# One numerator moved from the FFN chunks to the first down phase, whose tile pairs take their output projection last

## The chip, the cores and the metric

The kernel runs on one core of a Trainium2 chip. The metric is device time in microseconds (us), the median of repeated executions. TensorE appears in the profile as PE (matmuls) and PEld (weight loads), VectorE as DVE, ScalarE as ACT, GpSimd as POOL, and the queue that issues DMAs as SPq.

## The reference

A linear attention with softmax feature maps and a gated FFN share one input x of 2048 tokens by 640, and a per-token gate g mixes their outputs.

```python
qkv = x @ wqkv                       # 32 heads of 20
phi = concat[softmax(. @ w_phi), softmax(-. @ w_phi)]   # of q and of k
kv, z = phi_k^T v, sum(phi_k)        # per head
o = (phi_q kv) / (phi_q z + 1e-6)
a = o @ wo
b = (gelu(x @ w_gate) * (x @ w_up)) @ w_down            # F = 1728
out = g * a + (1 - g) * b,  g = sigmoid((x * gate_w).sum(-1))
```

## The kernel before, in words

Tokens are cut into 16 tiles of 128 and four blocks of four tiles (512 tokens). The attention state comes first (the first 80 us or so): projections, exponentials, their normalization and the key-value sums. Then `ffn` (line 752 on) runs two kinds of phase.

**Gate and up, `gateups(b)`**, four times, one for each block. Each runs 14 chunks of 128 FFN columns (`gateup`): five matmuls for the gate and five for the up product, 128 rows deep and 512 columns wide, into two PSUM banks, the pair (0, 1) or the pair (6, 7) in turn. ACT takes the gelu, DVE multiplies and leaves `hT`, the hidden values transposed.

**Down, `downs(b)`**, four times. Two tile pairs of a block follow each other, both through `down_pair` (line 696). A pair has an output of 640 columns, cut into two halves of 320 (h = 0 and 1); each half of each tile has a bank of its own: half 0 uses banks 0 and 1, half 1 uses banks 6 and 7, and the second pair, and the first pair of the next block, use the same four banks again. Every matmul here is only 64 rows deep, so two of them lie in the array beside each other: row half r = 0 works for one tile of the pair and r = 1 for the other. One such couple is a step here, and after each step the generator yields. A bank is filled in two turns: the opening, in which row half r works for tile r, and the closing, in which they change tiles, because the two row halves must not write one bank together. Before the closing writes a bank, PE waits for its own last opening matmul there (the key `turn`). The steps are 14 or 13 chunks of the down product (`wd_sb`, `hT`) and 5 chunks of the output projection (`wo_sb`, `goT`), which adds the attention's result to the same sums.

The order of a pair, before: opening down steps of half 0, then half 1 (14 + 14), opening projection steps (5 + 5), then the closing of half 0 with 13 down and 5 projection steps, its eviction, and the closing of half 1 with as many, its eviction. `evac` (line 722) evicts two banks, those of the two tiles, one after the other on ACT with the gate as scale (line 730), and issues the output DMA on SP after half 1.

**Numerators, `num(t)`** (line 647), one for each tile: 22 matmuls, 64 rows deep and 66 columns wide (line 662), into banks 2 to 5; then eleven DVE operations (lines 677 to 690), which read these banks and leave `Og`; then a transposing DMA on SP (line 693) that makes `goT`, which the projection steps of that tile read. `num` is called from hooks: `first_nums` after chunks of `gateups(1)`, and the dictionary `side` of `downs`, which maps a yield's count to a tile. Before, tiles 0 and 1 are made after chunks 4 and 8 of `gateups(1)`, and each down phase makes four at yields 1, 31, 61 and 91 (the last phase two). A phase has 148 yields.

The order within each engine is the program's; a scheduler object (`_Sched`, line 22) only adds the semaphore waits.

Of the kernel before, what the change touches and what calls it, by code (L numbers as in the profile page):

```python
# [107 lines left out]
class _Kernel:  # L108
# [6 lines left out]
    NFC = 14  # L115
# [279 lines left out]
    def mm(self, bank, c0, n, lhs, rhs, first, fin, reads):  # L395
        self.sc.op("pe", lambda e: e.matmul(  # L396
            self.ps[:, bank * 512 + c0:bank * 512 + c0 + n], lhs, rhs, start=first, stop=fin),
            reads=reads, writes=[("ps", bank)], signal=fin)
# [294 lines left out]
        sc.dma("sp", lambda e: e.dma_start_transpose(self.goT[:, gs, :, :], self.Og[:, sl, :]),  # L693
               reads=[("Og", sl)], writes=[("goT", gs)], guard=old)

    def down_pair(self, t0, banks, widths):

        sc = self.sc
        ts = (t0, t0 + 1)
        NFC, KD = self.NFC - 1, self.KD  # L700
        nw = len(widths)
        hk = t0 // 4
        last = t0 + 2 == self.NT
        os_ = t0 % 4

        def mm(r, j, h, c, opens, x, n):
            t = ts[j]
            tt, gs, bk, w0, a = t % 4, t % 8, banks[h][j], sum(widths[:h]), 64 * r
            w, end = widths[h], x == n - 1
            if c <= NFC:  # L710
                lhs, rhs = self.hT(hk, c)[a:a + 64, tt * P:(tt + 1) * P], self.wd_sb[a:a + 64, c, w0:w0 + w]
                rd = [("hT", hk, c), "wd"] if c < NFC else [("hT", hk, 13, r), ("wd13", r)]
            else:
                k = c - NFC - 1
                lhs, rhs = self.goT[a:a + 64, gs, k, :], self.wo_sb[a:a + 64, k, w0:w0 + w]
                rd = [("goT", gs), "wo"]
            sc.op("pe", lambda e: e.matmul(self.bank(bk, w), lhs, rhs, start=opens and x == 0, stop=end and not opens,  # L717
                                           skip_group_check=True),
                  reads=rd, writes=[("ps", bk)] + ([("turn", bk)] if end else []), signal=end,
                  after=[("turn", bk)] if x == 0 and not opens else ())  # L720

        def evac(h):
            w0, w = sum(widths[:h]), widths[h]
            for j in (0, 1):
                bk, dst, g = banks[h][j], self.outsb[:, os_ + j, w0:w0 + w], self.Gm[:, ts[j]:ts[j] + 1]
                rd, wr = [("ps", bk), "Gm"], [("outsb", os_ + j, h)]
                if last and j == 1:
                    sc.op("dve", lambda e: e.tensor_scalar(dst, self.bank(bk, w), g, None, op0=ALU.mult), reads=rd, writes=wr)
                else:
                    sc.op("act", lambda e: e.activation(dst, self.bank(bk, w), AF.Copy, scale=g), reads=rd, writes=wr)  # L730
            if last:
                hs, c0, c1 = [h], w0, w0 + w
            elif h == nw - 1:
                hs, c0, c1 = range(nw), 0, self.D
            else:
                return
            if t0 < self.TB:
                rows = self.out[0:self.BT, :].rearrange("(p j) n -> p j n", j=self.TB)[:, t0:t0 + 2, :]
            else:
                rows = self.out[t0 * P:(t0 + 2) * P, :].rearrange("(j p) n -> p j n", p=P)  # L740
            sc.dma("sp", lambda e: e.dma_start(rows[:, :, c0:c1], self.outsb[:, os_:os_ + 2, c0:c1]),
                   reads=[("outsb", os_ + j, k) for j in (0, 1) for k in hs], writes=[("out", t0, h)])

        wos = [NFC + 1 + k for k in range(KD)]
        opening = list(range(NFC + 1)) + wos
        for part in (range(NFC + 1), range(NFC + 1, len(opening))):
            for h in range(nw):
                for x in part:
                    for r in (0, 1):
                        mm(r, r, h, opening[x], True, x, len(opening))  # L750
                    yield None
        closing = list(range(NFC)) + wos
        for h in range(nw):
            for x, c in enumerate(closing):
                for r in (0, 1):
                    mm(r, 1 - r, h, c, False, x, len(closing))
                if c == closing[-1]:
                    evac(h)
                yield None

    NUMB = 2
    oldk = [("Ek", k, s) for k in range(5) for s in (0, 1)] + [(w, k) for w in ("Ekc", "Ekp") for k in range(5)] + [
# [5 lines left out]
    def ffn(self):  # L768
        self.gn = 0
        self.pn = 0  # L770
        pairs = [(0, 1), (6, 7)]

        def gateups(b, after):
            for idx, c in enumerate([0, 1, 13] + list(range(2, 13))):
                self.gateup(b, c, pairs[self.pn % 2])
                self.pn += 1
                after(idx)

        def downs(b, side):
            p = [pairs[(self.pn + k) % 2] for k in (0, 1)]  # L780
            n = 0
            for t in (4 * b, 4 * b + 2):
                final = t + 2 == self.NT
                for _ in self.down_pair(t, p + [(2, 3)] if final else p, (256, 256, 128) if final else (320, 320)):
                    n += 1
                    if n in side:
                        self.num(side[n])

        def state(idx):
            if idx < 4:  # L790
                self.gram(12 + idx)
            if idx == 3:
                self.kv_state()
                self.gates()

        def first_nums(idx):
            if idx in (4, 8):
                self.num(idx // 4 - 1)

        def none(idx):  # L800
            pass
        at = (1, 31, 61, 91)
        gateups(0, state)
        gateups(1, first_nums)
        gateups(2, none)
        gateups(3, none)
        for b in range(self.NB):
            downs(b, {at[k]: 4 * b + 2 + k for k in range(4 if b < 3 else 2)})


def bass_gated_mix__linear_kernel_hedgehog__geglu_ffn__prompt_kernel(
# [41 lines left out]
```

## Time and profile before

| what | value |
|---|---|
| median of 3 runs (lowest, highest) | 284.77 us (284.77, 285.49) |
| the profiled execution's own time | 284.86 us |
| its span | 283.5 us |
| granted TensorE clock | 1.00 |
| busy: PE, DVE, ACT, POOL | 280.3, 172.8, 104.8, 13.2 us |
| gateups(1) and its two numerators | about 107 to 138 us of the span |
| down phase of block 0 | 195.9 to 217.4 us |
| a down phase with four numerators | 21.48 us |

The profiled execution took 1.36 us more than its span; a change of the time is taken to be a change of the span. In a line of the timeline, the first number is the start in us from the span's start, the second how long the group lasted, then engine, line of the code, operation, tiles written and read, shape and count; brackets at the end give the idle time before it and what ended it. Matmuls are pipelined: a row of one lasts longer than the distance to the next, so distances between starts are what counts.

### The profile page before, as it was taken

What the parts mean: (1) busy time and instruction counts of PE and PEld (TensorE: products, weight loads), DVE (VectorE), ACT (ScalarE), POOL (GpSimd) and SP (SyncE); (2) the same over time, 40 slices, a digit from 0 to 9 for tenths busy, and PEclk for the clock granted to TensorE, in tenths of its full rate; (3) what the DMA queues carried; (4) which work ended last, traced back from release to release, by engine and by line L of the source; (5) the groups of instructions that cost most, each with busy time, mean ns of one, the idle gap of its engine ahead of it and who ended that gap; (6) DMA issues with size and microseconds to landing.
All of it is one profiled execution on the core that took longest, in us unless ns stands there. A gap on an engine that the chain in (4) does not pass through costs nothing.

```text
span 283.5 us, 6887 instructions
## 1 busy us (share of the span) xinstructions
PE 280.3 (99%) x2922; PEld 174.7 (62%) x2922; DVE 172.8 (61%) x325; ACT 104.8 (37%) x191; POOL 13.2 (5%) x67
## 2 busy tenths in 40 slices
PE   8999999999999999999999999999999999999996
PEld 5677777777754444444444444445777777777786
DVE  1369999999995332667242334325883883884801
ACT  4357888887852223222332223231112112012011
POOL 7500101110000000000000000000000000000000
DMA  8994398989999500011000000000133233232221
GB/s 227 189 219 91 60 198 179 192 180 165 171 250 353 146 0 0 2 23 24 2 0 0 0 2 0 0 0 2 25 50 85 58 44 76 72 44 76 73 73 49
DMA packets 58922, 24.11 MB, mean 85 GB/s; under 512 B 50954, under 2 KB 58378, under 8 KB 58890
## 3 DMA queue, kind: packets, MB, share of 16 engines
q1 hardware_dynamic: 58224, 23.63, 38.8%
q8 instruction: 23, 0.38, 0.6%
q10 hardware_dynamic: 666, 0.03, 0.2%
q14 instruction: 9, 0.07, 0.1%
HBM read 9.04 MB, written 2.62 MB: 41 GB/s over the span
## 4 chain that ended last, share of the span: by engine, by line
PE 94%; SPq 3%; DMA 2%; issue 0%; ACT 0%
PE ps L396 61%; PE ps L717 28%; PE ps L662 2%; DMA xT<-in_A_x_dram 2%; PE ps L506 2%; SPq L229 1%; SPq L245 1%; PE ps L374 1%; SPq L233 1%; SPq L225 0%; ACT outsb L730 0%
## 5 line engine op out<-in xcount | busy, mean ns | idle before, releaser
L396 PE MATMUL ps<-xT,wu_sb 128*128 128x512 bf16 x260 | 64.6, 379 | 0.0
L396 PE MATMUL ps<-xT,wg_sb 128*128 128x512 bf16 x260 | 64.6, 379 | 0.0
L633 ACT ACTIVATE gl<-ps 128x512 bf16<-128x512 f32 x52 | 31.1, 598 | 76.0 <-PE ps L396 73.8
L635 DVE TENSOR_TENSOR hT<-ps,gl 128x512 bf16<-128x512 f32 x39 | 26.7, 691 | 43.2 <-PE ps L396 43.2
L717 PE MATMUL ps<-wd_sb,hT 64*128 64x320 bf16 x648 | 48.4, 296 | 0.0
L396 PEld LDWEIGHTS ps<-xT,wu_sb 128*128 128x128 bf16 x260 | 25.4, 98 | 30.9 <-DVE hT L635 0.4
L396 PEld LDWEIGHTS ps<-xT,wg_sb 128*128 128x128 bf16 x260 | 25.0, 98 | 29.4
L730 ACT ACTIVATE outsb<-ps,Gm 128x320 bf16<-128x320 f32 (+2 forms) x31 | 14.6, 516 | 71.7 <-PE ps L717 71.7
L396 PE MATMUL ps<-w,xT 128*128 128x304 bf16 (+3 forms) x280 | 40.6, 296 | 0.3 <-DMA xT<-in_A_x_dram 0.3
L717 PEld LDWEIGHTS ps<-wd_sb,hT 64*128 64x128 bf16 x648 | 30.9, 94 | 12.2 <-issue 0.4
L396 PEld LDWEIGHTS ps<-w,xT 128*128 128x128 bf16 x280 | 26.4, 97 | 10.2 <-DMA xT<-in_A_x_dram 0.5
L717 PE MATMUL ps<-wo_sb,goT 64*128 64x320 bf16 (+2 forms) x340 | 26.5, 288 | 0.0
L495 DVE TENSOR_TENSOR Ek<-Ek,Dk 128x1320 bf16<-128x1320 bf16 x16 | 24.5, 1532 | 0.5
L688 DVE TENSOR_TENSOR O<-ps,RH 128x640 bf16<-128x640 f32 x32 | 24.8, 817 | 0.0
L486 DVE TENSOR_REDUCE Dk<-Ek 128x66 f32<-128x1320 bf16 x16 | 24.3, 1520 | 0.0
L396 PE MATMUL ps<-wq,xT 128*128 128x304 bf16 x160 | 23.3, 292 | 0.0
L453 ACT ACTIVATE Eqt<-ps 128x627 bf16<-128x627 f32 x32 | 20.5, 694 | 6.5 <-PE ps L396 6.5
L453 ACT ACTIVATE Ek<-ps 128x627 bf16<-128x627 f32 x32 | 20.5, 694 | 2.8 <-PE ps L396 2.6
L635 DVE TENSOR_TENSOR xT<-ps,gl 128x512 bf16<-128x512 f32 x13 | 9.0, 692 | 18.2 <-PE ps L396 18.2
L717 PEld LDWEIGHTS ps<-wo_sb,goT 64*128 64x128 bf16 x340 | 15.9, 94 | 5.3
L396 PEld LDWEIGHTS ps<-wq,xT 128*128 128x128 bf16 x160 | 15.0, 98 | 4.5
L717 PE MATMUL ps<-wd_sb,xT 64*128 64x320 bf16 (+2 forms) x270 | 16.0, 269 | 0.0
(77 smaller groups left out, 180.1 us busy)
## 6 DMA issues: line engine op xcount, KB each, us to landing
out_dram<-outsb SPq DMA_DIRECT2D x7, 320.0 KB, 2.3
wd_sb<-in_B_w_down_dram SPq DMA_DIRECT2D x1, 2080.0 KB, 10.6
wg_sb<-in_B_w_gate_dram SPq DMA_DIRECT2D x5, 224.0 KB, 4.0
wu_sb<-in_B_w_up_dram SPq DMA_DIRECT2D x5, 224.0 KB, 3.4
wg_sb<-in_B_w_gate_dram SPq DMA_DIRECT2D x5, 192.0 KB, 3.7
wu_sb<-in_B_w_up_dram SPq DMA_DIRECT2D x5, 192.0 KB, 3.3
w<-in_A_wqkv_dram SPq DMA_DIRECT2D x5, 160.0 KB, 4.0
wo_sb<-in_A_wo_dram SPq DMA_DIRECT2D x1, 800.0 KB, 9.6
```

The costliest lines, as they stand in the source:

```text
L229: sc.dma("sp", lambda e: e.dma_start_transpose(T[:, :, :], self.wqkv[:, c0:c0 + D]), writes=[key])
L396: self.sc.op("pe", lambda e: e.matmul(self.ps[:, bank * 512 + c0:bank * 512 + c0 + n], lhs, rhs, start=first, stop=fin), reads=reads, writ ...
L453: self.sc.op("act", lambda e: e.activation(dst, src, AF.Exp, scale=scale), reads=[("ps", b), ("ps", b + 1)], writes=[(name, sl, s)])
L486: self.sc.op("dve", lambda e: e.tensor_reduce(self.Dk[:, se, 0, :].rearrange("p (u h) -> p u h", h=self.HG), self.k_view(se), AX.X, ALU.ad ...
L495: sc.op("dve", lambda e: e.tensor_tensor(v, v, R.rearrange("p (u h) -> p u h", h=self.HG).unsqueeze(3).to_broadcast([P, 2 * self.G, self.H ...
L506: self.sc.op("pe", lambda e: e.matmul(self.bank(b)[:, c:c + n], self.Ek[:, se, g * P:(g + 1) * P], va[:, w * g:w * g + n], start=(t == 0 a ...
L633: sc.op("act", lambda e: e.activation(self.gl[:, slot, :], self.bank(banks[0]), AF.Gelu_apprx_tanh), reads=[("ps", banks[0])], writes=[("g ...
L635: sc.op("dve", lambda e: e.tensor_tensor(hT, self.bank(banks[1]), self.gl[:, slot, :], ALU.mult), reads=[("ps", banks[1]), ("gl", slot)], ...
L662: sc.op("pe", lambda e: e.matmul(self.ps[:, o:o + n], self.Eq[a:a + 64, g, t * P:(t + 1) * P], self.KV[a:a + 64, g, 0:n], start=(g in (0, ...
L688: dve(lambda e, o=o, f=f, s=s: e.tensor_tensor(o, V[s][:, :, 0:DH], f, ALU.mult), rb + [key(6 + s)], [("O", s, sl)], guard=old)
L717: sc.op("pe", lambda e: e.matmul(self.bank(bk, w), lhs, rhs, start=opens and x == 0, stop=end and not opens, skip_group_check=True), reads ...
L730: sc.op("act", lambda e: e.activation(dst, self.bank(bk, w), AF.Copy, scale=g), reads=rd, writes=wr)
```

## The change

Tile 0's numerator goes to the hook after chunk 8 of `gateups(1)`, the one after chunk 4 is gone, and the first down phase makes five numerators, tiles 1 to 5, at yields 1, 31, 61, 91 and 121. The other phases keep theirs. In the first down phase, for both tile pairs (`late=True`), the order becomes: opening down (14 + 14), closing down (13 + 13), opening projection (5 + 5), closing projection (5 + 5), with each half's eviction after its last step. The couple of row halves changes tiles three times in a pair, not once. The other three down phases keep their order.

```diff
-    def down_pair(self, t0, banks, widths):
+    def down_pair(self, t0, banks, widths, late=False):
...
-        def mm(r, j, h, c, opens, x, n):
+        def mm(r, j, h, c, begins, ends, opens, stops):
...
-            sc.op("pe", lambda e: e.matmul(self.bank(bk, w), lhs, rhs, start=opens and x == 0, stop=end and not opens,
-                                           skip_group_check=True),
-                  reads=rd, writes=[("ps", bk)] + ([("turn", bk)] if end else []), signal=end,
-                  after=[("turn", bk)] if x == 0 and not opens else ())
+            sc.op("pe", lambda e: e.matmul(self.bank(bk, w), lhs, rhs, start=opens, stop=stops, skip_group_check=True),
+                  reads=rd, writes=[("ps", bk)] + ([("turn", bk)] if ends else []), signal=ends,
+                  after=[("turn", bk)] if begins and not opens else ())
...
-        opening = list(range(NFC + 1)) + wos
-        for part in (range(NFC + 1), range(NFC + 1, len(opening))):
+        odown, cdown = list(range(NFC + 1)), list(range(NFC))
+        if late:
+            parts = [(0, odown), (1, cdown), (0, wos), (1, wos)]
+        else:
+            parts = [(0, odown), (0, wos), (1, cdown + wos)]
+        for k, (swap, steps) in enumerate(parts):
+            fin = k == len(parts) - 1
+            begins = k == 0 or parts[k - 1][0] != swap
+            ends = fin or parts[k + 1][0] != swap
             for h in range(nw):
-                for x in part:
+                for x, c in enumerate(steps):
+                    top, bot = x == 0, x == len(steps) - 1
                     for r in (0, 1):
-                        mm(r, r, h, opening[x], True, x, len(opening))
+                        mm(r, r ^ swap, h, c, begins and top, ends and bot, k == 0 and top, fin and bot)
+                    if fin and bot:
+                        evac(h)
                     yield None
-        closing = list(range(NFC)) + wos
-        for h in range(nw):
-            for x, c in enumerate(closing):
-                for r in (0, 1):
-                    mm(r, 1 - r, h, c, False, x, len(closing))
-                if c == closing[-1]:
-                    evac(h)
-                yield None
...
-                for _ in self.down_pair(t, p + [(2, 3)] if final else p, (256, 256, 128) if final else (320, 320)):
+                for _ in self.down_pair(t, p + [(2, 3)] if final else p, (256, 256, 128) if final else (320, 320), b == 0):
...
         def first_nums(idx):
-            if idx in (4, 8):
-                self.num(idx // 4 - 1)
+            if idx == 8:
+                self.num(0)
...
         at = (1, 31, 61, 91)
+        first = (1, 31, 61, 91, 121)
...
-            downs(b, {at[k]: 4 * b + 2 + k for k in range(4 if b < 3 else 2)})
+            if b:
+                downs(b, {at[k]: 4 * b + 2 + k for k in range(4 if b < 3 else 2)})
+            else:
+                downs(b, {first[k]: 1 + k for k in range(5)})
```

More of the change, by code (lines that the diff above doesn't have):

```diff
@@ L704, in down_pair @@
         os_ = t0 % 4
-        def mm(r, j, h, c, opens, x, n):
+        def mm(r, j, h, c, begins, ends, opens, stops):
             t = ts[j]
             tt, gs, bk, w0, a = t % 4, t % 8, banks[h][j], sum(widths[:h]), 64 * r
-            w, end = widths[h], x == n - 1
+            w = widths[h]
             if c <= NFC:
```

## The prediction

> **What bounds the kernel now.** I read the page's busy shares first, then the waits, then the timelines of the two stages that are touched.
>
> ```profile
> PE 280.3 (99%) x2922; PEld 174.7 (62%) x2922; DVE 172.8 (61%) x325; ACT 104.8 (37%) x191; POOL 13.2 (5%) x67
> ...
> PE 94%; SPq 3%; DMA 2%; issue 0%; ACT 0%
> ```
>
> PE is busy in 99% of the span, and the chain that ended last is PE for 94%. The list of waits gives PE one wait on a DMA (0.3 us) in the whole program and none in the down phases. So the change is worth what it does to the distances between PE's instructions: what PE no longer issues or drains is gained in full, and each new wait of PE is paid in full.
>
> What a numerator costs among FFN chunks (timeline of PE in gateups(1)):
>
> ```profile
> 115.91 1.24 PE L396 MATMUL ps<-xT,wu_sb 128*128 128x512 bf16 x5
> 117.08 0.51 PE L662 MATMUL ps<-KV,Eq 64*128 64x66 bf16 x22
> 117.53 1.25 PE L396 MATMUL ps<-xT,wg_sb 128*128 128x512 bf16 x5
> ```
>
> Five matmuls of a chunk take 1.08 us from start to start (118.62 less 117.53 is 1.09). Without the numerator the gate matmuls would have started at 116.99; they start at 117.53, 0.54 later, and the next five another 0.01 later. ACT agrees: its idle time before that chunk's gelu is 2.11 us where all others have 1.56, so 0.55 us.
>
> What one costs among down steps, which are 64 rows deep as it is, and what follows a half's last step there:
>
> ```profile
> 203.51 0.84 PE L717 MATMUL ps<-wo_sb,goT 64*128 64x320 bf16 x10
> 204.19 0.84 PE L717 MATMUL ps<-wd_sb,hT 64*128 64x320 bf16 x10
> 204.87 0.50 PE L662 MATMUL ps<-KV,Eq 64*128 64x66 bf16 x22
> 205.22 1.25 PE L717 MATMUL ps<-wd_sb,hT 64*128 64x320 bf16 x16
> ```
>
> Five steps take 0.68 us, so a step is 0.136; the numerator moves the next step by 205.22 - 204.87 = 0.35 us. The phase agrees: 148 steps of 0.136 and four times 0.35 make 21.5 us, and it takes 21.48.
>
> **The change part by part.**
>
> The numerator that moves. Removed: 0.55 us in gateups(1), since DVE's eleven operations delay no chunk that PE waits for (PE idles nowhere there). Added: 0.35 us in downs(0). Together -0.20 us.
>
> The order of a pair: as many steps as before (28 + 26 + 10 + 10 = 74), each with the same shapes, so nothing by count. More changes of tile, each with a wait for PE's own last matmul in the bank: the nearest is 5 steps back (0.68 us), and the same wait over 5 steps stands in the profile before (opening projection of half 1 between, closing starts at 201.75) without a gap in the rhythm. I cost it at nothing; if it cost what a matmul row lasts beyond its slot (0.30 - 0.14) it would be 0.16 us each, eight times, but no row hints at it.
>
> The eviction. This is the part that costs. Half 0's banks are evicted after its last step, and the next pair starts with half 0, on the same banks. Before, 18 steps of half 1 lie between (2.4 us); after, 5 steps (0.68 us). The eviction, from ACT's timeline:
>
> ```profile
> 204.42 0.95 ACT L730 ACTIVATE outsb<-ps,Gm 128x320 bf16<-128x320 f32 x2 [8.92 <-PE ps L717]
> 207.21 0.95 ACT L730 ACTIVATE outsb<-ps,Gm 128x320 bf16<-128x320 f32 x2 [1.84 <-PE ps L717]
> ```
>
> Let T be the start of half 0's last step. Here T = 204.19 - 0.136 = 204.05. ACT starts at T + 0.37; the first eviction lasts 0.52 (mean of the group) and ends at T + 0.89, the second ends with the group at T + 1.32. In the new order the next pair's first step would start at T + 6 x 0.136 = T + 0.81. Its first matmul needs the first bank, its second matmul the second. What it takes PE to resume is shown once: DVE's two products before 84.2 us end at 82.92 + 1.28 = 84.20, and the weight load that waited for them starts at 84.26, its matmul with it. I take 0.06 us. The first matmul then goes at T + 0.95, the second at T + 1.38, 0.57 us after its time. Both row halves are full in every step, so what the second half loses is not caught up: 0.57 us per place. Places: between the pairs of downs(0) (the waits of the changed program's order stand on the first two matmuls there, "ev_act"), and between downs(0) and downs(1), whose first pair takes the same banks. No numerator lies in either gap (they come after steps 61 and 121; the places are at 74 and 148). 2 x 0.57 = +1.14 us. Queued behind the waiting matmul is all of PE, which is the chain that ends last; half 1's banks are free 14 steps later, well after their eviction (T + 2.2). Bounds: nothing, if the release comes earlier than I read it; 2 x 0.75 if the resumption costs a drained matmul more (0.16).
>
> A rule stands against these stalls. The Trainium skill, "TensorE: Matmul & The Clock Gate", section "A second HAM failure mode: psum-queue depth-cycling", says that a PE that idles briefly between groups because it cycles through PSUM banks may fall back to half clock and warm up again. In this case's trace PE idled 0.4 us ahead of numerators twice, and the granted clock is 1.00; no run here shows a fallback. By the rule, with the page's window of about 3.4 us at half clock, an estimate is 1.7 us for each of the two places, and the sum would be 3.4 us larger; by the row nothing is added.
>
> Deadlines of `goT`. Tile 1 is now made at yield 1 and read at step 55. Its chain, from the numerator that stands at yield 1 before:
>
> ```profile
> 196.70 0.36 DVE L677 RECIPROCAL RH<-ps 128x32 f32<-128x32 f32 x1
> ...
> 200.41 0.49 DVE L690 TENSOR_TENSOR Og<-O,O 128x640 bf16<-128x640 bf16 x1
> ```
>
> Og is ready at 200.90, the DMA issues at 200.97. Step 55 is due at 195.89 + 54 x 0.136 + 2 x 0.35 = 203.93, its weight load 0.13 earlier, at 203.80. Nine of the sixteen transposes land 2.6 us after issue, which gives 203.57: 0.2 us in time. But seven took 3.5 to 5.0 us, this one among them:
>
> ```profile
> goT<-Og SPq DMA_TRANSPOSE x1, 4.3
> ```
>
> With 4.3 it lands at 205.27 and PE waits about 1.5 us. In the trace a 16 KB instruction transfer starts at 202.90 and lasts to 204.00, just as that transpose moves its data (202.15 to 203.08); the late ones all have such a transfer within theirs. These transfers follow PE's instruction count: at the same place in the down phase the changed program is one numerator (44 loads and matmuls, the length of 11 steps, 1.5 us) behind, so the transfer should start near 204.4, after the landing. I take 2.6, hence nothing, and keep 1.5 for the range. Tile 5, made at yield 121, is read 56 steps and a numerator later, 8.7 us after its matmuls start; its chain is 0.67 to DVE, 4.2 on DVE and 2.6 to land, 7.5: in time by about a microsecond.
>
> DVE and banks 2 to 5. The numerator of yield 121 is followed by the next after 28 steps, not 30: 28 x 0.136 + 0.35 = 4.16 us. DVE reads the banks until 4.3 us after the matmuls start, so a wait of about 0.2 us would be there, but the stall at the phase's end (0.57) stands ahead of it and covers it. If that stall is absent, this one takes its place.
>
> SP: the outputs' DMAs leave up to some 2 us later against `goT` of tiles 4 to 6, which have that much room; the last output DMA of the kernel is not touched.
>
> Sum: -0.20 + 1.14 = +0.94 us on the profiled execution's 284.86, 285.80 us, say 285.8. The median of the runs shown is 0.09 lower than the profiled execution, which I leave in the range.
>
> **The rivals.**
>
> A, a third wait: `goT` of tile 1 late (or tile 5). For it: seven of sixteen landings, and only 0.2 us of room. Against it: the instruction transfer should have moved away. Price up to 1.5 us more: 286.2 to 287.3.
>
> B, not slower: the wait of the second row half does not hold the stream. If PE goes on with the first row half's next steps, and the second's loss is taken up in the numerator or the change of tile that follow, only the first wait is paid, T + 0.95 against T + 0.81: 2 x 0.14 - 0.20 = +0.08; with the eviction's release hidden whole, -0.20 and the 0.2 us wait of the numerator back. 284.66 to 284.94. It decides from a stall per place under 0.10 us (no loss at all). For it: the row halves hold separate sums. Against it: every couple in the trace starts in the order of the program, and no row shows one half a step ahead.
>
> C, the change does not do what it says: the numerator is moved but the eviction stays where it was. The order listing of the changed program rules it out (40 projection matmuls in a row, then waits on ACT); I give it nothing.
>
> **How the numbers follow.** My sum 0.70, A 0.18, B 0.12. Within the sum's case the stall is known to some 0.1 us a place: 285.5 to 286.1. The range 285.3 to 286.5 holds this case and the smaller half of A, and leaves out B and the larger half of A, about 0.2. About 0.3% of this kernel's time, 0.85 us, is what a measurement can tell from no change. My sum of +0.94 lies just over it: I give slower 0.45 and same 0.25 of its 0.70; A is slower nearly whole (0.17, same 0.01); B is same (0.09) or, with a DVE queue that is better off than I see, faster (0.03). Slower 0.62, same 0.35, faster 0.03.
>
> **What would show it.** Right: two waits of PE (or PEld) on ACT's line of eviction, about 0.5 us each, at some 206 and 218 us; the chunks of gateups(1) with one numerator, 0.55 us sooner; no other new wait; ACT's two evictions of half 1 directly behind those of half 0. Wrong: a wait on the DMA of `goT` at step 55 (A); a wait on DVE ahead of the first numerator of downs(1), which would say that the stall before it is smaller than I think; a granted clock below 1.00; or couples of row halves that drift apart (B).

## The result and the profile after

The changed kernel takes 286.03 us in the median of 11 runs (285.60 to 287.35), before takes 285.28 (284.59 to 285.51): a ratio of 1.0039 over all executions of both, 95% interval 1.0025 to 1.0053, so some 1.1 us longer (0.7 to 1.5); the two medians alone lie 0.75 us apart. The forecast was 285.8, slower by 0.94 us. The slowdown is small, 0.4%, but the interval leaves out 1. The profiled execution took 285.61 us with a span of 284.3; before's took 284.86 with 283.5.

The page of the changed kernel, busy shares and the chain that ended last:

```profile
PE 280.8 (99%) x2922; PEld 189.7 (67%) x2922; DVE 173.0 (61%) x325; ACT 104.4 (37%) x191; POOL 13.2 (5%) x67
...
PE 93%; SPq 3%; DMA 2%; ACT 1%; issue 0%
```

PE still ends last, but ACT has come into the chain with 1% of the span; before it had 0%. The list of PEld's waits says where:

```profile
PEld ps L717 <- ACT outsb L729: 1.2, 4, 0.3
PEld ps L662 <- issue: 0.4, 1, 0.4
```

Four weight loads of the down phase wait for the eviction (line 729 is line 730 of before). The numerator's wait under "issue" (the profile shows nothing that it waited for) is 0.4 us once, where before had 0.8 in two: one numerator less among FFN chunks. The chunks around the place that became free are now in their plain rhythm of 1.08 us, and the one numerator left costs what it did (timeline of PE, changed kernel):

```profile
124.42 1.24 PE L396 MATMUL ps<-xT,wu_sb 128*128 128x512 bf16 x5
125.59 0.51 PE L662 MATMUL ps<-KV,Eq 64*128 64x66 bf16 x22
126.04 1.25 PE L396 MATMUL ps<-xT,wg_sb 128*128 128x512 bf16 x5
```

126.04 less (124.42 + 1.08) is 0.54. The first place between two pairs, in the timelines of PE, ACT and PEld:

```profile
204.54 1.93 PE L717 MATMUL ps<-wo_sb,goT 64*128 64x320 bf16 x26
206.44 2.90 PE L717 MATMUL ps<-wd_sb,hT 64*128 64x320 bf16 x34
```

```profile
205.86 1.78 ACT L729 ACTIVATE outsb<-ps,Gm 128x320 bf16<-128x320 f32 x4 [11.03 <-PE ps L717]
217.13 1.78 ACT L729 ACTIVATE outsb<-ps,Gm 128x320 bf16<-128x320 f32 x4 [9.49 <-PE ps L717]
```

```profile
206.44 0.09 PEld L717 LDWEIGHTS ps<-wd_sb,hT 64*128 64x128 bf16 x1 [0.30 <-ACT outsb L729]
206.86 0.79 PEld L717 LDWEIGHTS ps<-wd_sb,hT 64*128 64x128 bf16 x14 [0.33 <-ACT outsb L729]
```

Read together: the 26 projection matmuls are 13 steps from 204.54, so the next step was due at 204.54 + 13 x 0.136 = 206.31. Its first weight load starts at 206.44 (0.13 late, first bank released), its second at 206.86 (0.55 late, second bank). ACT now does all four evictions of a pair in one row; before it did two and two, 2.4 to 2.8 us apart. The second place is the same, at the end of the phase:

```profile
217.71 0.09 PEld L717 LDWEIGHTS ps<-wd_sb,hT 64*128 64x128 bf16 x1 [0.27 <-ACT outsb L729]
218.13 0.09 PEld L717 LDWEIGHTS ps<-wd_sb,hT 64*128 64x128 bf16 x1 [0.33 <-ACT outsb L729]
```

The time can be laid out by two distances between starts in the trace. From the first FFN matmul to the last: 118.89 us before, 118.35 after, -0.55. From the last FFN matmul to the end of the last matmul: 85.81 before, 87.26 after, +1.45, which is 0.35 for the fifth numerator and 1.10 for two waits. Together +0.90. The span grew by 0.75 only, because the first FFN matmul of this execution happened to start 0.13 us earlier (76.55 against 76.68), in a stage that the change does not touch; this start lay between 76.55 and 77.62 us in the profiles here, and so the second distance is what the kernels below are compared by. (The other profiles lack the record of that very first matmul, so that in them the first distance is counted from the next one, some 0.2 us later; it is compared among them alone: 118.68 us in late_only, which keeps both numerators among the chunks, and 118.12 or 118.13 in those that have one, again 0.55 less.) It is 87.25 to 87.26 in the three profiles of the changed kernel.

### The profile page after: what moved, and what is told of

It reads as the page before. It is cut to its first block, busy times and chain, and to the rows that moved or that the text cites. A ratio compares the mean times of both kernels' runs of the same rounds, so it can differ in the third digit from the quotient of the medians.

```text
span 284.3 us, 6890 instructions
## 1 busy us (share of the span) xinstructions
PE 280.8 (99%) x2922; PEld 189.7 (67%) x2922; DVE 173.0 (61%) x325; ACT 104.4 (37%) x191; POOL 13.2 (5%) x67
## 4 chain that ended last, share of the span: by engine, by line
PE 93%; SPq 3%; DMA 2%; ACT 1%; issue 0%
PE ps L396 61%; PE ps L717 28%; PE ps L662 2%; PE ps L506 2%; DMA xT<-in_A_x_dram 2%; SPq L229 1%; ACT outsb L729 1%; SPq L245 1%; SPq L233 1%; PE ps L374 1%; SPq L225 0%
## 5 line engine op out<-in xcount | busy, mean ns | idle before, releaser
L717 PE MATMUL ps<-wd_sb,hT 64*128 64x320 bf16 x648 | 50.1, 296 | 0.2
L717 PEld LDWEIGHTS ps<-wd_sb,hT 64*128 64x128 bf16 x648 | 40.7, 94 | 4.6 <-ACT outsb L729 1.2
L717 PE MATMUL ps<-wo_sb,goT 64*128 64x320 bf16 (+2 forms) x340 | 27.2, 288 | 0.0
L717 PEld LDWEIGHTS ps<-wo_sb,goT 64*128 64x128 bf16 x340 | 21.0, 94 | 1.1
```

## The experiments

All times are against before, on the same chip in the same set. "Down distance" is that from the last FFN matmul to the end of the last matmul in the kernel's profile.

| kernel | ratio, 95% interval | down distance, us | less before's 85.81 |
|---|---|---|---|
| changed kernel, 2nd set | 1.0037 (1.0024 to 1.0050) | 87.26 | +1.45 |
| changed kernel, 3rd set | 1.0037 (1.0022 to 1.0052) | 87.25 | +1.44 |
| late_only | 1.0042 (1.0029 to 1.0054) | 86.90 | +1.09 |
| move_only | 1.0001 (0.9992 to 1.0011) | 86.39 | +0.58 |
| move_only_30 | 0.9990 (0.9978 to 1.0003) | 86.18 | +0.37 |
| evict_twice | 1.0091 (1.0066 to 1.0116) | 88.37 | +2.56 |
| gap_ten | 1.0032 (1.0020 to 1.0043) | 87.23 | +1.42 |
| second_pair | 1.0047 (1.0035 to 1.0060) | 87.64 | +1.83 |
| filler | 1.0017 (1.0006 to 1.0029) | 87.07 | +1.26 |
| tile1_free | 1.0034 (1.0022 to 1.0046) | 87.26 | +1.45 |
| tile1_free, 2nd set | 1.0031 (1.0019 to 1.0043) | 87.25 | +1.44 |

**The order alone.** All numerators where before has them, the late order kept:

```diff
-            if idx == 8:
-                self.num(0)
+            if idx in (4, 8):
+                self.num(idx // 4 - 1)
...
-            if b:
-                downs(b, {at[k]: 4 * b + 2 + k for k in range(4 if b < 3 else 2)})
-            else:
-                downs(b, {first[k]: 1 + k for k in range(5)})
+            downs(b, {at[k]: 4 * b + 2 + k for k in range(4 if b < 3 else 2)})
```

> The late order in the first down phase, but all numerators where before has them (tiles 0 and 1 among the FFN chunks). Theory: the two waits are all the order costs, +1.12 us against before, 0.2 more than the changed kernel's quiet executions. Rival A: tile 1's transposed result is ready long before, so the tail of slow executions is gone and the median lies under that of the changed kernel by some 0.1 to 0.3. Rival (the order's additional changes of tile cost too): more than +1.12, with gaps at the starts of the parts.

Measured: +1.09 us in the down distance, and in PEld's waits the same row as the changed kernel's:

```profile
PEld ps L717 <- ACT outsb L729: 1.2, 4, 0.3
```

The order costs its two waits and nothing else; the additional changes of tile between row halves leave no gap. By the time it is 1.2 us (0.8 to 1.5) slower, as the theory has it. What rival A expected did not come: the median, 286.05, does not lie under that of the changed kernel in the same set, 285.92, and two of six executions (286.46 and 286.61) lie 0.85 and 1.00 us above the quickest.

**The move alone.** The order of before everywhere; tiles 1 and 3 read their neighbours' `goT`:

```diff
                 k = c - NFC - 1
+                gs = t - 1 if t in (1, 3) else gs
...
-                for _ in self.down_pair(..., b == 0):
+                for _ in self.down_pair(..., False):
```

> The numerators where the changed kernel has them, but the order of steps of before in all down phases; tiles 1 and 3 would be read too early then, so their projection steps read the transposed result of tiles 0 and 2 in place of their own (this part of the result is left out). Theory: -0.20 us for the numerator that moved, and +0.2 for DVE's hold on banks 2 to 5 ahead of the first numerator of the second down phase, which comes 28 steps after the one before; no wait on ACT. Together 0.0 against before. Rival (a numerator costs the same in either place): +0.2. Rival (the hold is not there): -0.2.

and the same with the second down phase's numerators two steps later:

```diff
-                downs(b, {at[k]: 4 * b + 2 + k for k in range(4 if b < 3 else 2)})
+                downs(b, {at[k] + 2 * (b == 1): 4 * b + 2 + k for k in range(4 if b < 3 else 2)})
```

> The same, with the numerators of the second down phase two steps later (3, 33, 63, 93), so that 30 steps lie between all. Theory: the wait on DVE goes and the move alone is left, -0.20 us against before in the time, and in the trace 0.55 less between the first FFN chunk and the last, 0.35 more from there to the end. Rival (a numerator costs the same in either place): 0.0.

Measured: +0.58 and +0.37 us in the down distance. The second is the numerator's price there, 0.35 forecast; the difference of 0.21 is DVE's hold on banks 2 to 5, which the first kernel has in its list of waits and the second has not:

```profile
PEld ps L662 <- DVE O L688: 0.4, 1, 0.4
```

(PEld is idle for 0.4 us there; what PE loses by it is the 0.21.) Less the 0.55 saved among the chunks (118.12 us in both kernels), the sums are +0.03 and -0.18. The times, 1.0001 and 0.9990, agree, though the interval of the second takes in 1: a gain of 0.18 us is under what these runs can tell. The rival, that a numerator costs the same in either place, falls by the trace.

**A longer eviction.** The second eviction of half 0 is done twice:

```diff
-                    sc.op("act", lambda e: e.activation(dst, self.bank(bk, w), AF.Copy, scale=g), reads=rd, writes=wr)
+                    for _ in range(2 if late and h == 0 and j == 1 else 1):
+                        sc.op("act", lambda e: e.activation(dst, self.bank(bk, w), AF.Copy, scale=g), reads=rd, writes=wr)
```

> The changed kernel, with the second eviction of half 0 done twice in both pairs of the first down phase, which releases the second bank one ACT interval (0.43 us) later. Theory: PE waits for the second bank's release, so each of the two waits grows by 0.43, +0.85 on the changed kernel, about +1.8 against before. Rival B (only the first wait counts): no change against the changed kernel.

Measured: +1.11 us on the changed kernel's down distance. The direction and the place are the theory's, the size was 0.43 a place in the expectation and is 0.56. ACT's row shows where the rest comes from:

```profile
205.98 2.34 ACT L730 ACTIVATE outsb<-ps,Gm 128x320 bf16<-128x320 f32 x5 [11.02 <-PE ps L717]
```

Five evictions take 2.34 where four took 1.78: two evictions in a row overlap (their starts are 0.43 apart, each lasts 0.52), but the repeated one, which writes what the first wrote, has a wait for it in the program and starts at 206.96, after the first has ended at 206.93. PE follows the second release one for one:

```profile
206.56 0.31 PE L717 MATMUL ps<-wd_sb,hT 64*128 64x320 bf16 x1
207.54 0.72 PE L717 MATMUL ps<-wd_sb,hT 64*128 64x320 bf16 x8 [0.67 <-ACT outsb L730]
```

The first matmul goes with the first release, 0.13 late as before; everything behind it waits for the second. Rival B, that only the first wait counts, is out.

**A wait taken away, and what came in its place.** In the second pair, half 0 is finished 18 steps before the end. The parts become a list of (half, swap, steps), and the loop over them, not shown, is rewritten to suit:

```diff
+            parts = [(h, s, p) for s, p in ((0, odown), (1, cdown), (0, wos), (1, wos)) for h in range(nw)]
+            if t0 == 2:
+                parts = [(0, 0, odown), (1, 0, odown), (0, 1, cdown), (0, 1, wos),
+                         (1, 0, wos), (0, 0, wos), (1, 1, cdown), (1, 1, wos)]
...
```

> The changed kernel, but in the second pair of the first down phase half 0 is finished 18 steps before the pair's end (half 0: down, down, projection, projection; half 1's closing last), so that its eviction is over when the next phase wants its banks. Theory: the second wait on ACT (0.56) goes; DVE's hold on banks 2 to 5 then shows as a wait of about 0.2 ahead of the first numerator of the next phase, since that numerator comes 28 steps after the one before; together 0.35 less than the changed kernel, about +0.55 against before. Rival (the wait at the phase's end is hidden or not the eviction's): no gain.

Measured: not 0.35 less than the changed kernel but 0.38 more. PEld's waits, this kernel:

```profile
PEld ps L717 <- DMA goT<-Og: 0.9, 1, 0.9
PEld ps L717 <- ACT outsb L729: 0.6, 2, 0.3
...
PEld ps L662 <- DVE O L688: 0.4, 1, 0.4
```

Both expected things are there: the waits on ACT are down from four to two, from 1.2 to 0.6 us, and the wait on DVE has appeared. But a third was not expected: the projection steps now start at step 42 of the pair, and the transposed result of tile 3 came too late for them. Its issue, and when PE went on:

```profile
goT<-Og SPq DMA_TRANSPOSE x1, 4.3
```

```profile
213.75 0.99 PE L717 MATMUL ps<-wo_sb,goT 64*128 64x320 bf16 x12 [0.53 <-DMA goT<-Og]
```

Issued at 209.41, it landed 4.3 us later, at 213.71; with 2.6 us it would have been there at 212.0, a microsecond before it was wanted. A 16 KB instruction transfer began at 211.15, while the transpose's data moved (most of it from 210.59 to 211.40), and lasted to 212.10; eighteen packets of the transpose that had started by 211.40 ended only at 212.91 to 212.94. So 0.55 + 0.35 + 0.2 of the distance's +1.83 are known, and some 0.7 us is this wait. It is the wait that rival A had in mind, at another tile.

**Other ways of ending a pair.** Half 0 takes both projection parts in a row, then half 1:

```diff
+            parts = [(h, s, p) for s, p in ((0, odown), (1, cdown)) for h in range(nw)]
+            parts += [(0, 0, wos), (0, 1, wos), (1, 0, wos), (1, 1, wos)]
...
```

> The changed kernel, but at the end of both pairs of the first down phase half 0 takes both its projection parts in a row, then half 1 both of its own: ten steps (1.36 us) between half 0's eviction and the next pair, where the second release needs 1.37 less one step. Theory: the waits on ACT go (1.12 us), but now the closing part follows the opening part on the same bank at once, so PE waits for its own last matmul there, about 0.22 us (0.30 of a matmul, 0.06 to resume, less the 0.14 of a step), four times: 0.9 in place of 1.12, and 0.2 for DVE's hold on banks 2 to 5 at the next phase, no gain or loss beyond 0.2 against the changed kernel. Rival (a change of tile costs nothing even back to back): 0.9 less than the changed kernel.

Measured: 0.03 us less than the changed kernel. The waits on ACT are gone, and these stand in their place:

```profile
PEld ps L717 <- PE ps L717: 1.7, 4, 0.4
```

Four waits of PE for its own last matmul in the bank. The down distance less the numerator leaves 1.07, so each costs 0.27 us (0.22 expected), and the wait on DVE did not show, as the numerator of the next phase is later by these waits. A change of tile is free with five steps between, and costs 0.27 us with none.

And the next phase's first numerator put into the gap:

```diff
-                downs(b, {at[k]: 4 * b + 2 + k for k in range(4 if b < 3 else 2)})
+                downs(b, {at[k]: 4 * b + 2 + k for k in range(b == 1, 4 if b < 3 else 2)})
             else:
-                downs(b, {first[k]: 1 + k for k in range(5)})
+                downs(b, {(first + (148,))[k]: 1 + k for k in range(6)})
```

> The changed kernel, with the numerator of tile 6 one step earlier: at the end of the first down phase, between half 0's eviction and the next pair's first step, not after that step. Theory: PE does the numerator's 0.35 us while it would wait for ACT; DVE's hold on banks 2 to 5 lets it start about 0.2 us after the phase's end, and both banks are free when it is through, so some 0.3 us less than the changed kernel, about +0.6 against before. Rival (the wait for the eviction starts only where PE comes to it, and the numerator merely moves it): no change.

Measured: 0.19 us less than the changed kernel, where 0.3 was expected:

```profile
218.01 0.52 PE L662 MATMUL ps<-KV,Eq 64*128 64x66 bf16 x22 [0.15 <-DVE O L688]
218.37 3.96 PE L717 MATMUL ps<-wd_sb,hT 64*128 64x320 bf16 x56
```

The numerator runs in the time of the eviction and no wait on ACT is left at this place. But DVE's hold costs more than 0.2 us: the numerator was due at 214.89 + 20 x 0.136 = 217.61 and starts at 218.01, 0.40 late. Most of the difference is a slip of the expectation, which took over the 0.2 of a numerator 28 steps after the one before; here there are 27, 27 x 0.136 + 0.35 = 4.02 us, against 4.29 + 0.06 for which the banks are held in before, so 0.33. The rest is that since the first wait the second row half runs a step behind the first: the numerator at yield 121 ends later, and DVE starts 0.75 us after its first matmul, in before 0.67. Of the versions with the late order it has the lowest ratio, and is still slower than before (1.0017); no version that computes the whole beats before.

**Rival A, tile 1's transposed result.** Four of the changed kernel's first 11 executions took 286.88 to 287.35, 1.2 us and more above the quickest. The kernel repeated, and one in which tile 1's projection reads tile 0's `goT`:

```diff
                 k = c - NFC - 1
+                gs = 0 if t == 1 else gs
```

> The changed kernel once more, beside the others. Theory (two waits for the eviction of 0.56 us each, less 0.20 us for the numerator that moved): +0.9 us against before in its quiet executions, with waits of PE on ACT's eviction at two places. Rival A (the transposed attention result of tile 1 comes too late in some executions): beside these quiet ones, a share of executions 1.2 to 1.6 us longer still, as 4 of the 11 known ones were (286.88 to 287.35 against 285.60 to 286.12). If that tail comes from the chip's state, before has it too.

> The changed kernel, but tile 1's projection steps read tile 0's transposed attention result in place of its own, so that nothing waits for tile 1's; all instructions stay. Theory without rival A: nothing changes, +0.9 in quiet executions and the same tail. Rival A: the quiet executions stay and the tail 1.2 to 1.6 us above them vanishes.

> The changed kernel a third time, for its slow tail: 4 of the first 11 executions were 1.2 us and more above the fastest, 0 of 5 in the second set. Theory: +0.9 against before. Rival A would show here as executions at 286.9 and above, and not in the kernel whose tile 1 waits for nothing.

> The kernel whose tile 1 reads tile 0's transposed result (its own is left out), again, for the tail. Rival A: no execution at 286.9 or above while the changed kernel has some. Theory without it: no difference between the two.

Measured: the changed kernel 285.69 to 286.18 in five executions, and 285.68 to 286.36 with one of 287.01 in six; the other one 285.63 to 286.25 in eleven. In every profile of the changed kernel the transpose of tile 1 landed in 2.6 us; in the first it was there at 202.88, and PE loads the weights at 203.11. So five of 22 executions have the tail, and none of eleven without the dependency; if both had the same share, that would still come about once in nine times. No profile caught one of them, and before has single executions at 286.42 and 286.47.

For rival A: the instruction transfer starts very near the landing. In the three profiles of the changed kernel it starts at 203.12, 203.19 and 203.10, the transpose having landed at 202.88, 203.04 and 203.11, so a little earlier would be enough to meet it. Against it: gap_ten and filler have the same order up to where tile 1 is read, and none of their 21 executions has the tail (at most 286.43); late_only, whose tile 1 is ready at 133.92, has some spread of its own; and evict_twice has two of six at 288.13 and 288.80, 1.0 us and more above its others (286.90 to 287.12), which tells nothing about the cause. That the tail is tile 1's transpose, late by an instruction transfer, is possible and not shown.

## Why the prediction was right, point by point

- The numerator that moves, -0.55 and +0.35: -0.55 in the trace, +0.37 in move_only_30.
- The order by itself at nothing, changes of tile five steps apart included: late_only has only the two waits.
- The eviction, 0.57 us at two places, decided by the second bank: 0.55 at both; late_only 1.09 for two, and evict_twice moves it one for one. The resumption of 0.06 us, read from a single wait on DVE, held for ACT (0.05: the second eviction ends at 206.81, the load starts at 206.86).
- The deadline of tile 1, 0.2 us to spare: 0.23 in the profile. That no instruction transfer met its transpose was nearly luck. The prediction had it start near 204.4, 0.8 us after the landing, in a phase that began at 195.89; that is 8.5 us after the phase's start, 1.5 later than in before (7.0). It moved by 0.6 to 0.9 only (7.7 to 7.9 in the three profiles), which brought it to within 0.24 us of the landing. The sum holds, as these profiles have no such wait, but the room that it took for granted was not there. Tile 5 was in time by 0.96 us (landed at 221.09, weights loaded at 222.05).
- DVE's hold of about 0.2 us, covered by the stall: no wait in the changed kernel, 0.21 us in move_only, where nothing covers it.
- The fallback of the clock, which the Trainium skill allows ("TensorE: Matmul & The Clock Gate", section "A second HAM failure mode: psum-queue depth-cycling"), did not come: PEld idled 0.3 us four times here and PE 0.67 us at once in evict_twice, and the granted clock is 1.00 in every profile. (The 0.4 us that the prediction gives to PE ahead of numerators are idle time of PEld; the list of waits has none of PE there.)
- Rival B was half right in its picture, wrong in its price. The first row half does run on, and stays a step ahead of the second, of which the trace of before had shown nothing. But the second half is full as well, so it sets the end, and the loss is the whole 0.55.
- The sum: +0.94 forecast, +0.90 in the two distances of the trace, +1.1 (0.7 to 1.5) by the times. That the median came so near the forecast, 286.03 against 285.8, is in part chance: before took 285.28 in that set and not the 284.86 that the forecast starts from, and four of the eleven executions are the tail, whose cause stays open; the other seven have a median of 285.70.

## What to carry to other kernels

Where a matmul stream reuses its banks, count the steps between an eviction and the next write of the bank, and compare them with the eviction's end: here 18 steps hid it, 5 did not, and the last bank released is the one that counts. A move that saves 0.2 us is soon spent by the reordering that it needs: price the reordering first. And a wait taken away shows the next one behind it (DVE's hold), and a read moved forward can meet a new one (the transposed result), so the slack of each must be known before the gain is written down.

## What the runs showed of the hardware that had not been expected

After a wait that holds only one of two 64-row halves, the other half is one step ahead and keeps that lead: the first half's matmul of the step starts at 206.44, the second's at 206.86 together with the first half's next, and in the rows after 209 us a numerator's 22 matmuls no longer stand together but mix with a down step. The changed kernel:

```profile
209.05 0.55 PE L662 MATMUL ps<-KV,Eq 64*128 64x66 bf16 x19
209.42 0.30 PE L717 MATMUL ps<-wd_sb,hT 64*128 64x320 bf16 x1
209.44 0.24 PE L662 MATMUL ps<-KV,Eq 64*128 64x66 bf16 x3
```

The lead stays until the numerator at 265.65. PEld's busy time rises with it from 174.7 to 189.7 us for the same 2922 loads of the same mean length, since the loads of the two halves lie less upon each other; it costs nothing by itself. The transposes of `goT` land late where a transfer of instructions runs beside them. In the thirteen profiles 90 of 208 landed 2.9 to 5.5 us after their issue, and all of these had such a transfer while their data moved; the other 118 took 2.6 us, and 111 of them had none and seven one that began in their last 0.3 us. In second_pair PE paid some 0.7 us for one of them. No run moves such a transfer by itself, so that it is the cause is not tested.
